# First batch of a fused linear-attention and MLP kernel: order of the kv and x products, a one-column mean operand, evictions split over two engines, float32 fill matmuls

## The chip, the cores and the metric

The kernel runs on one core of one Trainium2 chip. The metric is the device time of one execution, in microseconds (us), smaller being better. Instructions run on five engines, each with its own queue in program order: PE (TensorE, matmuls; PEld in the profile is its loading of the stationary operand, which runs beside the matmul before it), DVE (VectorE), ACT (ScalarE), POOL (GpSimd) and SP (SyncE). POOL and SP mostly issue DMA transfers here.

## What is computed

```
q_s = softmax(q, over head_dim)            # 8 batches, 8 heads, 576 tokens, 64
k_s = softmax(k, over the tokens)
kv  = einsum('bhsd,bhse->bhde', k_s, v)    # one 64 x 64 matrix per head
x   = einsum('bhsd,bhde->bhse', q_s, kv)   # heads side by side: 576 x 512
xn  = (x - mean(x)) / sqrt(var(x) + 1e-6) * g_ln
out = x + relu(xn @ w_ch1) @ w_ch2         # 512 x 2048 and 2048 x 512
```

## The kernel before

Each batch has 576 tokens: 512 are handled batch by batch in four tiles of 128 tokens (t = 0 to 3), and the last 64 of all batches together at the end. Two heads share a block of 128 columns, so there are four head pairs (j = 0 to 3) and four blocks of 128 rows of w_ch1 (ko = 0 to 3). All of the work is put in order by hand: `run` walks the list of main matmul steps of a batch and calls side work at given places in it. After the first batch, PE has work nearly all the time.

The change lies in `first_batch` (line 957), which does what comes before the first MLP, and in the helpers it calls:

- **Loads.** SP issues the first two token tiles of q and then k (lines 978 to 982). POOL first copies four numbers of q into `gate` (line 1004), so that its own transfers start when that q has landed, and then issues in this order: v in three parts (line 1006: heads 0 to 3, 4 and 5, 6 and 7), q tiles 2 and 3 (line 970), the first 512 columns of w_ch1 in two halves of K (line 1013: ko 0 and 1, then ko 2 and 3; tile `w_raw`), the other column blocks of w_ch1 (line 99), w_ch2 (line 103) and batch 1.
- **Fill.** `warm(n)` (line 863) issues n matmuls of 128x512 on the zeroed tile `junk`, with nothing depending on them.
- **q.** `exp_qt` (ACT, line 220), then for tiles 0 and 1 `norm_q` (DVE, lines 229, 274, 923), then `eq_pT`: four PE transposes into the PSUM tile `ptr` (line 928) and a copy to `eqT` on DVE (line 934) or ACT (line 930). Tiles 2 and 3 are not divided by their sums; those come later from `z_q` (PE line 940, DVE line 943).
- **k and kv.** `exp_k0` (ACT, line 293), `z0_mm` (PE, line 306: the sums of k), `g_columns` (line 953, a float32 matmul that transposes g), `recip_z`. `kv0_mm(j)` does six matmuls for a head pair (line 321); DVE scales and masks the result into `kv_sb` and sums its rows into a column (line 322). That column is then spread into a 128x128 tile `mbc`: by ACT (line 327) for j = 0 to 2, by DVE (line 331) for j = 3. `mbc` is all `-1/512` (`ones_w`) times the sum, so that a matmul with it as stationary operand subtracts the mean of x.
- **x, transposed.** `xT_mm(j, kh)` (line 342) adds pair j's share to one PSUM tile `pxT` for each half kh of the 512 columns of x: one matmul with `kv_sb` where the pair belongs to the half, and two with `mbc`. `xT_out(i)` multiplies block i by g and writes `xnT`, the moving operand of the MLP: on DVE for i = 0, 1 (line 351), on ACT for i = 2, 3 (line 353). This gives tokens 0 to 255.

The order on PE is kv0_mm(0), (1), (2), xT_mm(0, 0), kv0_mm(3), xT_mm(1, 0), (2, 0), (0, 1), (3, 0), the transposes of q tile 2, xT_mm(1, 1), (2, 1), the transposes of q tile 3, xT_mm(3, 1). ACT evicts the transposes of tile 2, DVE those of tile 3.

Then `run(mlp_steps(0), ...)` starts. Its first main steps are matmuls of line 520 with the first 512 columns of w_ch1: eight with ko 0 and 1, then eight with ko 2 and 3. Between them PE does, in this order: after four matmuls `q0_rest(2)` (lines 940, 943, 414), followed on DVE by `x_fast(0, 2)` (line 464) and `x_normed(2)` (line 475); after eight, `q0_rest(3)`; after twelve, the transposes of the normalized tile 2 (line 928 into `ptr`, evicted by DVE at line 932), then `x_fast` and `x_normed` of tile 3. The next main steps are sixteen matmuls of 128 columns for tile 2, the transposes of tile 3, and sixteen matmuls with the second column block of w_ch1.

Of the kernel before, what the change touches and what calls it, by code (L numbers as in the profile page):

```python
# [12 lines left out]
FP32 = mybir.dt.float32  # L13
BF16 = mybir.dt.bfloat16
AF = mybir.ActivationFunctionType
# [5 lines left out]
def kernel(  # L21
# [16 lines left out]
    nc = tc.nc  # L38

    B, H, S, D = q.shape  # L40
    DM = H * D
    DH = 4 * DM
    P = 128
    T = 4
# [4 lines left out]
    NP = H // 2  # L49
# [10 lines left out]
    const = ctx.enter_context(tc.tile_pool(name="const", bufs=1))  # L60
# [12 lines left out]
    eps_ln = const.tile([P, 1], FP32)  # L73
    gate = const.tile([P, 4], FP32)
    ones = const.tile([P, 1], BF16)
    junk = const.tile([P, P], BF16)
    scrap = const.tile([P, 512], BF16)
    bones = const.tile([P, 2], BF16)
    ones_w = const.tile([P, P], BF16)
    diag = const.tile([P, P], FP32)  # L80
    mbc = const.tile([P, NP, P], BF16)
    g_one = const.tile([P, KO1], FP32)
    w1_sb = wts.tile([P, KO1, DH], BF16, name="w1_raw")
    w1g = const.tile([P, KO1, DH], BF16)
# [12 lines left out]
    def load_w1(nb):  # L97
        cols = slice(nb * 512, nb * 512 + 512)
        nc.gpsimd.dma_start(w1_sb[:, :, cols], w1_src[:, :, cols])
# [100 lines left out]
    def new_eq(c):  # L200
        eqs[c] = (
            att.tile([P, T, H, D], BF16, tag="eq", name="eq", bufs=1),
            sml.tile([P, T, H], FP32, tag="zq", name="zq"),
            sml.tile([P, T, H], FP32, tag="rq", name="rq"),
        )
        eqTs[c] = att.tile([P, T, NP, P], BF16, tag="eqT", name="eqT")
# [10 lines left out]
    def exp_qt(b, t):  # L217
        if t == 0 and b:
            new_eq(b)
        nc.scalar.activation(eqs[b][0][:, t], raws[b][2][:, :, t], AF.Exp)  # L220
# [66 lines left out]
    kvbox = {}  # L287
# [9 lines left out]
    def k0_mm(j, t):  # L297
        hs = slice(2 * j, 2 * j + 2)
        return eks[0][0:P0, t, hs, :], raws["v0"][0:P0, hs, t, :], P
# [16 lines left out]
    def kv0_mm(j):  # L316
        pool, tag = (att_ps, "a") if j < 2 else (mm_ps, "m")
        pkv = pool.tile([P, P], FP32, tag=tag, name="pkv")
        for t in range(T0):
            lhsT, rhs, w = k0_mm(j, t)  # L320
            nc.tensor.matmul(pkv[:, 0:w], lhsT, rhs, start=(t == 0), stop=(t == T0 - 1))
        nc.vector.scalar_tensor_tensor(
            kv_sb[:, 0, j, :], in0=pkv, scalar=kvbox["rz"][:, j : j + 1], in1=diag,
            op0=ALU.mult, op1=ALU.mult, accum_out=kvbox["sum"][:, j : j + 1],
        )
        if j < NP - 1:
            nc.scalar.activation(
                mbc[:, j], ones_w, AF.Copy, scale=kvbox["sum"][:, j : j + 1]
            )
        else:  # L330
            nc.vector.tensor_scalar_mul(
                out=mbc[:, j], in0=ones_w, scalar1=kvbox["sum"][:, j : j + 1]
            )

    def xT_mm(j, kh):

        if j == 0:
            pobox["T", kh] = mm_ps.tile([P, 2, 2, P], FP32, tag="m", name="pxT")
        ops = [(kv_sb[:, 0, j, :], j % 2)] if j // 2 == kh else []
        ops += [(mbc[:, j], i) for i in range(2)]  # L340
        for n, (lhsT, i) in enumerate(ops):
            nc.tensor.matmul(
                pobox["T", kh][:, i], lhsT, eqTs[0][:, 0:2, j, :],
                start=(j == 0 and n == 0), stop=(j == NP - 1 and n >= len(ops) - 2),
                skip_group_check=True,
            )

    def xT_out(i):
        dst, src = xnTs[0][:, 0:2, i, :], pobox["T", i // 2][:, i % 2]
        if i < 2:  # L350
            nc.vector.tensor_scalar_mul(out=dst, in0=src, scalar1=g_one[:, i : i + 1])
        else:
            nc.scalar.activation(dst, src, AF.Copy, scale=g_one[:, i : i + 1])
# [509 lines left out]
    def warm(n):  # L863

        w = mm_ps.tile([P, 4, P], FP32, tag="m", name="warm")
        for _ in range(n):
            nc.tensor.matmul(w, junk, junk[:, 0:4].to_broadcast([P, 4, P]), start=True, stop=True)
# [57 lines left out]
    def pe_T(dst, src, t, eng, scale=None):  # L925
        ptr = mm_ps.tile([P, NP, 2 * P], BF16, tag="m", name="ptr")
        for j in range(NP):
            nc.tensor.transpose(ptr[:, j, 0:P], src[:, j * P : j * P + P], ident)  # L928
        if eng is nc.scalar:
            nc.scalar.copy(dst[:, t], ptr[:, :, 0:P])  # L930
        elif scale is not None:
            nc.vector.tensor_mul(dst[:, t], ptr[:, :, 0:P], scale.to_broadcast([P, NP, P]))
        else:
            nc.vector.tensor_copy(out=dst[:, t], in_=ptr[:, :, 0:P])
# [10 lines left out]
    def eq_pT(c, t, eng):  # L945
        pe_T(eqTs[c], eqs[c][0][:, t].rearrange("p h d -> p (h d)"), t, eng)
# [10 lines left out]
    def first_batch():  # L957

        nc.scalar.preload_act_table_set("natural_log_exp_and_others")
        raws[0] = (  # L960
            mlp.tile([P, H, T0, D], FP32, tag="hT", name="kt0", bufs=1), None,
            raw.tile([P, H, T, D], FP32, tag="qt", name="qt"),
        )
        k0, _, q0 = raws[0]
        v0 = mlp.tile([P, H, T0, D], BF16, tag="hs", name="v0", bufs=1)
        raws["v0"] = v0

        def load_q0(t, tn, eng):
            ts = slice(t, t + tn)
            eng.dma_start(  # L970
                q0[:, :, ts],
                q[0, :, 0:SM, :].rearrange("h (p t) d -> p h t d", t=T)[:, :, ts],
            )

        def src0(x, h0, hn):
            return x[0, h0 : h0 + hn].rearrange("h (p t) d -> p h (t d)", t=T0)

        load_q0(0, 2, nc.sync)
        for h0 in range(0, H, 2):
            nc.sync.dma_start(  # L980
                k0[0:P0, h0 : h0 + 2].rearrange("p h t d -> p h (t d)"), src0(k, h0, 2)
            )
        raws["g"] = outp.tile([KO1, P], FP32, tag="ot", name="g_rows")
        nc.scalar.dma_start(
            raws["g"], bass.AP(moe_g_ln.tensor, moe_g_ln.offset, [[P, KO1], [1, P]])
        )
        nc.vector.memset(junk, 0.0)
        nc.vector.memset(eps_ln, 1e-6)
        nc.vector.memset(ones, 1.0)
        nc.vector.memset(bones, 0.0)  # L990
        nc.vector.memset(bones[0:64, 0:1], 1.0)
        nc.vector.memset(bones[64:P, 1:2], 1.0)
        nc.vector.memset(ones_w, -1.0 / DM)
        nc.vector.memset(diag, 0.0)
        for ps in halves:
            nc.vector.memset(diag[ps, ps], 1.0)
        nc.vector.memset(kv_sb[:, 1:B], 0.0)
        nc.vector.memset(vr, 0.0)
        for half in range(2):
            nc.vector.memset(vr[64 * half : 64 * half + 64, :, 4 * half : 4 * half + 4, D:], 1.0)  # L1000
        nc.vector.memset(vm[:, :, :, :, D:], 1.0)
        make_identity(nc, ident)
        nc.gpsimd.tensor_copy(out=ident_f, in_=ident[0:KO1, 0:KO1])
        nc.gpsimd.tensor_copy(out=gate, in_=q0[:, 1, 0, 0:4])
        for h0, hn in ((0, 4), (4, 2), (6, 2)):
            nc.gpsimd.dma_start(  # L1006
                v0[0:P0, h0 : h0 + hn].rearrange("p h t d -> p h (t d)"), src0(v, h0, hn)
            )
        for t in range(2, T):
            load_q0(t, 1, nc.gpsimd)  # L1010
        for kh in range(2):
            ks = slice(2 * kh, 2 * kh + 2)
            nc.gpsimd.dma_start(w1_sb[:, ks, 0:512], w1_src[:, ks, 0:512])
        for nb in range(1, 4):
            load_w1(nb)
        load_w2(0)
        load_w2(1)

        new_eq(0)
        start_x(0)  # L1020
        warm(17)
        for t in range(2):
            exp_qt(0, t)
            norm_q(0, t)
        eq_pT(0, 0, nc.vector)
        warm(6)
        eq_pT(0, 1, nc.vector)
        for j in range(NP):
            exp_k0(j)
            z0_mm(j)  # L1030
            if j == NP - 2:
                g_columns()
        recip_z()
        kv0_mm(0)
        kv0_mm(1)
        kv0_mm(2)
        xT_mm(0, 0)
        kv0_mm(3)
        exp_qt(0, 2)
        exp_qt(0, 3)  # L1040
        xT_mm(1, 0)
        xT_mm(2, 0)
        xT_mm(0, 1)
        xT_mm(3, 0)
        xT_out(0)
        xT_out(1)
        eq_pT(0, 2, nc.scalar)
        xT_mm(1, 1)
        xT_mm(2, 1)
        eq_pT(0, 3, nc.vector)  # L1050
        xT_mm(3, 1)
        xT_out(2)
        xT_out(3)

    def q0_rest(t):
        z_q(0, t)
        for i in range(NP):
            po_mm(0, t, i)
# [132 lines left out]
```

## Time and profile before

The medians and the profile are of the same kernel; the profiled execution is one more run.

| | us |
|---|---|
| median of 3 runs (lowest, highest) | 262.51 (261.97, 262.89) |
| profiled execution | 262.09 |
| its span, first to last instruction | 260.3 |
| PE busy in the span | 253.9 (98%) |
| DVE, ACT, POOL busy | 223.1 (86%), 177.5 (68%), 103.2 (40%) |
| PE instructions (matmuls; loads) | 2885; 2885 |

Times of rows are counted from the start of the span. A row of a timeline has start, length, engine, line, operation, `out<-in`, shape and count; in square brackets stands how long the engine had been idle before and what ended it. The length of a matmul row includes the time in which its result drains, while the next matmul already runs, so the distance between two starts tells what a matmul costs in a stream: 0.109 us for 256 columns, 0.056 for 128, 0.025 for one or two columns.

### The profile page before, as it was taken

The page shows a single profiled execution, that of the slowest core. Times are in us where ns is not written, and L with a number is a line of the kernel's source. Part 1 is how long each engine was busy: PE and PEld are TensorE (multiplying, and loading weights), DVE is VectorE, ACT ScalarE, POOL GpSimd, SP SyncE. Part 2 cuts the span into 40 slices and gives each one's busy share as a digit, 9 for nine tenths or more (in the row PEclk, how much of TensorE's full clock was granted, in tenths as well). Part 3 has the DMA queues.
Part 4 walks back from the last instruction along what each step waited for, and adds up shares of the span by engine and source line. Part 5 has one row for each costly group of instructions (what it writes and reads, how often), then busy time and mean ns, then how long its engine had stood idle before and what let it go on. Part 6 is the DMA issues. An engine that isn't in the chain of part 4 may idle for free.

```text
span 260.3 us, 7286 instructions
## 1 busy us (share of the span) xinstructions
PE 253.9 (98%) x2885; PEld 215.6 (83%) x2885; DVE 223.1 (86%) x542; ACT 177.5 (68%) x348; POOL 103.2 (40%) x160
## 2 busy tenths in 40 slices
PE   8899999999999999999999999999999999999993
PEld 3689755788888888888888988888889888888883
DVE  6768996989989998899889988998899889957873
ACT  4747790997988685888588858885788386647400
POOL 3953247410299409800980098008200900190000
PEclk9999999999999999999999999999999999999999
DMA  6999999988699995999699859989902630422014
GB/s 198 257 203 208 354 221 332 257 169 308 118 122 321 268 120 107 300 247 107 142 300 235 86 135 304 232 89 161 279 0 50 142 137 1 77 71 99 3 40 121
DMA packets 82618, 45.04 MB, mean 173 GB/s; under 512 B 58196, under 2 KB 79192, under 8 KB 82584
## 3 DMA queue, kind: packets, MB, share of 16 engines
q0 software_dynamic: 32464, 21.76, 45.8%
q1 hardware_dynamic: 49488, 22.29, 36.8%
q10 hardware_dynamic: 632, 0.53, 0.7%
q8 instruction: 22, 0.36, 0.6%
q14 instruction: 12, 0.10, 0.1%
HBM read 36.70 MB, written 9.44 MB: 177 GB/s over the span
## 4 chain that ended last, share of the span: by engine, by line
PE 92%; DMA 4%; POOL 2%; DVE 0%; issue 0%
PE ba L604 21%; PE bx L762 20%; PE bb L762 10%; PE ph L520 8%; PE bb L604 6%; PE be L604 5%; PE bc L604 5%; PE pc L556 5%; PE bc L762 5%; DMA w_raw<-in_moe_w_ch_dram 3%; PE pkv L371 2%; DMA qt<-in_q_dram 2%; PE po L403 2%; PE ptr L928 1%; PE po L414 1%; POOL v L1006 1%
## 5 line engine op out<-in xcount | busy, mean ns | idle before, releaser
L604 PEld LDWEIGHTS <-hs 128*128 128x128 bf16 x512 | 49.6, 98 | 6.0
L269 POOL TENSOR_TENSOR tq<-xnT 128x256 bf16<-128x256 bf16 x30 | 20.1, 671 | 85.3 <-PE bc L604 73.9
L762 PEld LDWEIGHTS <-w_raw 128*128 128x128 bf16 x480 | 46.7, 98 | 5.5
L604 PEld LDWEIGHTS <-hT 128*128 128x128 bf16 x392 | 37.6, 98 | 4.2
L762 PEld LDWEIGHTS <-w1g 128*128 128x128 bf16 x360 | 34.7, 98 | 4.3 <-issue 0.2
L762 PE MATMUL bx<-tq,w_raw 128*128 128x256 bf16 x240 | 31.3, 273 | 0.0
L604 PE MATMUL ba<-w_q,hs 128*128 128x256 bf16 x256 | 30.6, 273 | 0.0
L786 ACT COPY bc<-bx 128x512 f32<-128x512 f32 x30 | 16.7, 596 | 19.1 <-PE bx L762 19.1
L427 ACT ACTIVATE scrap<-x,mv 128x512 bf16<-128x512 bf16 x32 | 23.1, 723 | 4.6 <-DVE mv L457 4.4
L793 DVE TENSOR_TENSOR bb<-bx,s 128x512 f32<-128x512 f32 x30 | 19.5, 694 | 7.2 <-ACT s L790 4.5
L804 ACT ACTIVATE hT<-bb 128x512 bf16<-128x512 f32 x30 | 16.3, 595 | 9.3 <-PE bb L762 9.3
L804 ACT ACTIVATE hT<-bc 128x512 bf16<-128x512 f32 x30 | 16.5, 595 | 8.5 <-PE bc L762 8.5
L796 DVE TENSOR_TENSOR hT<-bx,s 128x512 bf16<-128x512 f32 x30 | 19.3, 684 | 3.2 <-PE bx L762 3.1
L587 DVE TENSOR_TENSOR hs<-hT 128x1024 bf16<-128x1024 bf16 x32 | 21.4, 672 | 0.5 <-ACT hT L804 0.5
L229 DVE TENSOR_REDUCE zq<-eq 128x16 f32<-128x1024 bf16 (+1 forms) x20 | 20.7, 1049 | 0.5 <-ACT eq L220 0.5
L269 POOL TENSOR_TENSOR tq<-xnT,tq 128x256 bf16<-128x256 bf16 x30 | 20.0, 669 | 1.1
L449 DVE SCALAR_TENSOR_TENSOR x<-po,rq 128x256 bf16<-128x256 f32 x48 | 17.5, 420 | 1.7 <-PE po L403 1.7
L790 ACT COPY s<-bb 128x512 f32<-128x512 f32 x30 | 16.6, 622 | 0.0
L804 ACT ACTIVATE hT<-bx 128x512 bf16<-128x512 f32 x30 | 16.4, 610 | 0.0
L762 PE MATMUL bx<-xnT,w1g 128*128 128x256 bf16 x120 | 16.2, 273 | 0.0
L762 PE MATMUL bx<-tq,w1g 128*128 128x256 bf16 x120 | 15.9, 272 | 0.0
L762 PE MATMUL bc<-xnT,w1g 128*128 128x256 bf16 x120 | 15.8, 273 | 0.0
(157 smaller groups left out, 535.0 us busy)
## 6 DMA issues: line engine op xcount, KB each, us to landing
out_dram<-ot POOLq DMA_DIRECT2D x30, 256.0 KB, 4.4
kt<-in_k_dram SPq DMA_DIRECT2D x5, 1024.0 KB, 11.6
qt<-in_q_dram SPq DMA_DIRECT2D x4, 1024.0 KB, 9.9
qt<-in_q_dram POOLq DMA_DIRECT2D x2, 1024.0 KB, 12.7
kt<-in_k_dram POOLq DMA_DIRECT2D x2, 1024.0 KB, 14.5
vm<-in_v_dram POOLq DMA_DIRECT2D x16, 128.0 KB, 12.4
qt<-in_q_dram SPq DMA_DIRECT2D x3, 512.0 KB, 5.7
w_raw<-in_moe_w_ch_dram POOLq DMA_DIRECT2D x3, 512.0 KB, 10.5
```

Of the source, the lines that this page charges most:

```text
L229: nc.vector.reduce_sum(eqs[c][1][:, ts], eqs[c][0][:, ts], axis=AX.X)
L269: nc.gpsimd.tensor_tensor(out=dst[:, t], in0=x[:, t], in1=y[:, t], op=ALU.subtract)
L427: nc.scalar.activation(scrap, x[:, t], AF.Square, bias=mv[:, t, 0:1], scale=-float(DM), accum_out=mv[:, t, 1:2],)
L449: nc.vector.scalar_tensor_tensor(x[:, t].rearrange("p (i two d) -> p i two d", two=2, d=D)[:, :, half], in0=pobox[c, t][half], scalar=1.0, ...
L520: nc.tensor.matmul(ph[:, m % 2, at : at + tn], (w1g if c else w1_sb)[:, ko, m * P : (m + 1) * P], xnTs[c][:, t0 : t0 + tn, ko, :], start=( ...
L587: nc.vector.tensor_tensor(out=dst, in0=x, in1=y, op=op)
L604: nc.tensor.matmul(hbox[bank][:, t, cs], lhsT, rhs[:, cs], start=first and (own or t == 0) and k == 0, stop=k == KH - 1, skip_group_check= ...
L762: nc.tensor.matmul(dst[:, q], lhsT, rhs, start=first and q == 0 and ko == 0, stop=ko == 1, skip_group_check=True)
L786: nc.scalar.copy(at[g, "c"], at[g, "x"])
L793: nc.vector.tensor_tensor(out=at[g, "b"], in0=at[g, "x"], in1=at[g, "s"], op=ALU.add)
L796: nc.vector.tensor_tensor(out=h_out(g, 1, 1), in0=at[g, "x"], in1=at[g, "s"], op=ALU.add)
L804: nc.scalar.activation(h_out(g, odd, half), at[g, name], AF.Relu)
```

## The change

It touches the first batch alone.

- The fill matmuls use a float32 `junk`; there are 4 and 1 of them in place of 17 and 6.
- The mean is kept as one column per pair (`kvm`, the sum times -1/512), and a matmul reads that column 128 times with step 0 as its stationary operand; the 128x128 tiles `mbc` and `ones_w` go.
- All four `kv0_mm` come ahead of every `xT_mm`; the `xT_mm` of half 0 come together, then those of half 1, and the transposes of q tiles 2 and 3 come after both.
- In each half DVE evicts the first block and ACT the second.
- `exp_qt(0, 3)` comes after the evictions of half 0 on ACT, and DVE evicts the transposes of both q tiles.

```diff
-    junk = const.tile([P, P], BF16)
+    junk = const.tile([P, P], FP32)
...
-    ones_w = const.tile([P, P], BF16)
...
-    mbc = const.tile([P, NP, P], BF16)
+    kvm = const.tile([P, NP], BF16)
...
+        total = kvbox["sum"][:, j : j + 1]
         if j < NP - 1:
-            nc.scalar.activation(
-                mbc[:, j], ones_w, AF.Copy, scale=kvbox["sum"][:, j : j + 1]
-            )
+            nc.scalar.activation(kvm[:, j : j + 1], total, AF.Copy, scale=-1.0 / DM)
         else:
-            nc.vector.tensor_scalar_mul(
-                out=mbc[:, j], in0=ones_w, scalar1=kvbox["sum"][:, j : j + 1]
-            )
+            nc.vector.tensor_scalar_mul(out=kvm[:, j : j + 1], in0=total, scalar1=-1.0 / DM)
...
-        ops += [(mbc[:, j], i) for i in range(2)]
+        ops += [(kvm[:, j : j + 1].to_broadcast([P, P]), i) for i in range(2)]
...
-        if i < 2:
+        if i % 2 == 0:
...
-        nc.vector.memset(ones_w, -1.0 / DM)
...
-        warm(17)
+        warm(4)
...
-        warm(6)
+        warm(1)
...
-        kv0_mm(0)
-        kv0_mm(1)
-        kv0_mm(2)
-        xT_mm(0, 0)
-        kv0_mm(3)
+        for j in range(NP):
+            kv0_mm(j)
         exp_qt(0, 2)
-        exp_qt(0, 3)
-        xT_mm(1, 0)
-        xT_mm(2, 0)
-        xT_mm(0, 1)
-        xT_mm(3, 0)
+        for j in range(NP):
+            xT_mm(j, 0)
         xT_out(0)
         xT_out(1)
-        eq_pT(0, 2, nc.scalar)
-        xT_mm(1, 1)
-        xT_mm(2, 1)
-        eq_pT(0, 3, nc.vector)
-        xT_mm(3, 1)
+        exp_qt(0, 3)
+        for j in range(NP):
+            xT_mm(j, 1)
         xT_out(2)
         xT_out(3)
+        for t in range(2, T):
+            eq_pT(0, t, nc.vector)
```

## The prediction

> **What bounds the kernel now.** First the page: which engine is full, and which ends the chain.
>
> ```profile
> PE 253.9 (98%) x2885; PEld 215.6 (83%) x2885; DVE 223.1 (86%) x542; ACT 177.5 (68%) x348; POOL 103.2 (40%) x160
> ...
> PE 92%; DMA 4%; POOL 2%; DVE 0%; issue 0%
> ```
>
> PE bounds the time, so an edit pays only if PE begins its long run earlier or stands still less. The share that is not PE lies at the start, so the second view is the chain that ended last, in order of time (start, length):
>
> ```profile
> 7.33 1.84 POOL qt L970 x2
> 9.18 0.64 POOL w_raw L1013
> 9.82 6.86 DMA w_raw<-in_moe_w_ch_dram
> 16.72 0.61 PE ph L520 x4
> ```
>
> Up to 16.72 us nothing that PE, DVE or ACT computes is on the chain. It waits for the second half of the first w_ch1 block, which POOL issues at 9.82 and which lands at 16.68. All edits lie before that. The third view, the PE timeline, tells how much earlier PE could have gone on:
>
> ```profile
> 11.31 0.27 PE L342 MATMUL pxT<-eqT,kv_sb 128*128 128x256 bf16 x1
> 11.60 0.39 PE L342 MATMUL pxT<-eqT,mbc 128*128 128x256 bf16 x2
> 11.83 0.50 PE L321 MATMUL pkv<-v,ek 96*128 96x128 bf16 x6
> ...
> 15.93 0.38 PE L414 MATMUL po<-kv_sb,eqT 128*128 128x128 bf16 x4
> 16.72 0.61 PE L520 MATMUL ph<-xnT,w_raw 128*128 128x256 bf16 x4 [0.41 <-DMA w_raw<-in_moe_w_ch_dram]
> ```
>
> The last `po` starts at 16.09, so PE is free at 16.15 and 0.57 us are lost. The fourth, DVE's timeline, shows the chain behind the stall:
>
> ```profile
> 15.34 0.21 DVE L943 RECIPROCAL rq<-zs 128x8 f32<-128x8 f32 x1 [0.42 <-PE zs L940]
> 15.66 0.69 DVE L464 SCALAR_TENSOR_TENSOR x<-po,rq 128x512 bf16<-128x512 f32 x1
> 16.28 0.08 DVE L464 DVE_READ_ACCUMULATOR x<-po,rq 128x1 f32 x1
> 16.40 0.35 DVE L475 TENSOR_SCALAR xn<-x,st 128x512 bf16<-128x512 bf16 x1
> ...
> 17.60 0.69 DVE L932 TENSOR_TENSOR xnT<-ptr,g_col 128x512 bf16<-128x512 bf16 x1 [0.73 <-PE ptr L928]
> ```
>
> `xn` of tile 2 is ready at 16.75, before PE asks for it at 17.17. From there DVE and PE alternate until 19.57, where the second w_ch1 block is needed; it landed at 19.26.
>
> Last, the DMA view of 15 to 17 us:
>
> ```profile
> q0 software_dynamic: 394, 0.40, 120.8%
> q8 instruction: 1, 0.02, 3.0%
> ```
>
> The engines are full. Of the sixteen landing marks of that `w_raw` half, fifteen are there by 15.71; the last comes at 16.68. The packet in q8 has 16 KB, starts at 15.90 and takes 0.95 us. There are 22 such packets for 5784 PE records, one per 263, and this first one starts when PE has begun 260. I read it as PE's own instructions, fetched on an engine that still had weights to deliver. For the half before, the last mark came 0.18 behind the next to last; undisturbed, this one would be there at 15.71 + 0.18 = 15.89.
>
> **Fill.** 23 bf16 matmuls become 5 in float32. Nothing depends on them, and after each lot PE waits for DVE (line 923 ends at 7.36 and 8.92). The one float32 matmul of the trace, `gcp`, makes two records, each with a load of 0.18 us. So `warm(4)` is 8 records. A 512-column record costs 0.427 before 4.2 us (distance of the loads) and 0.218 after. With one pass per record the fill, begun at 1.0, ends at 4.5; with two at 6.1, as it does now (6.3); all slow, at 7.9. The first two are hidden; the last delays the first transposes by 0.5, but DVE copies those at 8.84 only. I take 0, with two passes, since 16 passes are nearest to the 17 of now. The Trainium skill, FP8 and Floating Point Precision, "TensorE Precision Notes", has true FP32 take four passes, which would be two per record; no run shows it yet, and the sum would stay as it is. What counts is that 46 fill records become 20: PE's stream is 26 shorter.
>
> **Mean column.** ACT's three `mbc` (1.17 together) become 128x1 operations: not under 0.2 (line 505, 128x4: 0.21), not over 0.39; I take 0.21. DVE's 0.25 becomes 0.14 (line 482, 128x1). A load with step 0 is not in the trace: 0.098 as other loads (nothing to gain, it lies under the matmul before it, 0.109), at most 0.18 as float32. I take 0.098; the tile is bf16 as they are. At 0.18, sixteen loads cost 16 x 0.07 = 1.1. The `ones_w` memset (0.17) goes and `junk` takes 0.06 more; both are hidden by the first q transfer (5.03).
>
> **The new order**, from the same rows. Part 3 of v lands at 11.72, so `kv0_mm(3)`, before at 11.83, starts at 11.77 and PE idles from 11.31, where `xT_mm(0, 0)` stood: the order gives that filling away. Last kv matmul 12.05; `kv_sb(3)` 0.25 later, 12.31 to 12.67 with its sum; `kvm(3)` at 12.84. `xT` half 0 runs from 12.11, ten at 0.109, its last start at 13.09, result 0.31 later at 13.40 (before 13.51). DVE and ACT evict side by side, to 13.86. `exp_qt(0, 2)` (q landed at 12.42, 0.72) is done by 13.16; `exp_qt(0, 3)` runs behind the eviction, 13.78 to 14.50 (before 13.84). `xT` half 1: last start 14.18, evicted 14.49 to 14.95. Transposes of tile 2 from 14.29, of tile 3 from 14.56. DVE has `xT_out(2)` ahead of them: copies to 15.29 and 15.63 (before 14.92 for the later). Then PE: four `ph` 14.79 to 15.23, waits for `eqT` of tile 2, `zs` and `po` 15.34 to 15.66, four `ph` to 16.10, `zs` and `po` of tile 3 to 16.42. So PE is free at 16.42, 0.27 **later** than before; the DMA wait covers that. On DVE: `rq` 15.62, `x` 15.87, its sum to 16.57, `xn` 16.62 to 16.97 (before 16.75). Queued behind it is only `rq` of tile 3. No DMA is moved; POOL and SP issue as before, and batch 1's k, which reuses the tile of `ek`, is queued to 15.09 behind POOL's own issues.
>
> **The instruction packet.** In the old stream its trigger lies some time before 15.90, say at record 210 to 245 (14.1 to 15.4). The same place in the new stream is 26 records later in the work, at 15.4 to 16.5: the packet starts at about 17, and `w_raw` lands at 15.9. Then PE goes on at 16.42 and reaches the transposes of tile 2 at 16.86, where `xn` (16.97, plus 0.05) is late next: 17.02 in place of 17.17. All behind moves by 0.15, to 19.42 at the second block, which may still land at 19.26 with the packet on its engine.
>
> The Trainium skill, Runtime: NRT & Kernel Launch, "Instruction fetch mechanics", calls the cost of crossing an instruction block mostly hidden. For PE's own issue that agrees with this trace; the 0.8 us on the weights' last mark (16.68 - 15.89) speaks against it. By that rule alone the change would give 0.
>
> **Sum.** Fill 0, column 0, order 0 (its +0.27 is under the wait), packet -0.15: the profiled execution goes from 262.09 (span 260.3 and 1.8 around it, unchanged) to 261.94. The median shown is 0.42 above that execution; 262.51 - 0.15 = 262.36.
>
> **Rivals.**
> - *The transfer hides everything.* The packet still meets the same half, landing stays at 16.68, PE (16.42) and `xn` (16.97, asked at 17.17) stay under it: 262.5. For it: the trigger is inferred. 0.26.
> - *Slower: the clock.* Loads stand 0.427 apart until 3.96 and 0.218 from 4.31: PE runs at half speed until it has worked some 3.2 us. If float32 fill does not count as work, the rise comes 3.2 us after the dense matmuls begin at 10.2. Then 3.2 us of work, half done, lose 1.6; 0.3 of slack before 16.72 and some 0.3 of v's wait take up 0.6: +1.0, 263.5. It decides as soon as more than 0.6 us are lost. If it comes only after the line 520 stream, some +4.5. Against it: two passes per record keep PE as busy as now. 0.10. The Trainium skill, TensorE: Matmul & The Clock Gate, "Part 1: The HAM clock gate", has the full rate return after one busy window of about 3.4 us and be lost after an idle one; the rise at 4.2 us agrees.
> - *Slower: the step-0 load* is at 0.18: PE free at 17.5, +0.8, 263.3. It costs from 0.02 per load on (0.3 / 16). 0.05.
> - *Later packets.* All 21 others move by 26 records; each can hold a transfer for 0.9 us or free one. Either sign, mostly under 0.5; PE has some 3 us of stalls behind 19.6 in all. 0.17: 0.07 faster by over 0.8, 0.03 slower by that, the rest between.
>
> **Numbers.** Forecast 0.42. 0.3% is 0.79 us, about what a measurement of this kernel can tell from no change. Faster: 0.07, and 0.02 for a forecast whose DVE chain is shorter than worked out: 0.09. Slower: 0.10 + 0.05 + 0.03 = 0.18, less 0.01 for the load's lower half: 0.17. Same: 0.74. Range: forecast and first rival with 0.7 either way, and up to the near end of the clock rival: 261.6 to 263.4.
>
> **What would show it.** Right: no PE row with a DMA wait at 16.7; line 520's second lot at about 16.4; line 928 on `xn` at 17.0; the q8 packet after 16.4. The order: `pkv` idle before 11.77, `pxT` half 0 done at 13.4, DVE's `eqT` copies at 14.9 and 15.2. Step-0 loads of 98 ns. Ten float32 records, full rate by 4.2 us. Wrong: 16.72 unchanged; matmuls 0.21 apart behind 10 us; loads over 0.12; any new PE idle behind 20 us.

## The result, and the profile after

The changed kernel takes 263.94 us (median of 7 runs, 263.21 to 264.76), the kernel before 262.44 on the same chip: ratio 1.006 [1.0037, 1.0083]. It is slower by 1.5 us where 262.36 was forecast; the forecast range ended at 263.4. The profiled execution took 264.76, with a span of 263.0.

The page of the changed kernel, first as a whole: busy time, the granted clock in 40 slices, and the two queues that carry data (packets, MB, share of 16 engines' time).

```profile
PE 256.1 (97%) x2872; PEld 216.7 (82%) x2872; DVE 223.4 (85%) x542; ACT 176.6 (67%) x347; POOL 103.1 (39%) x160
...
PEclk9979999999999999999999999999999999999999
...
q0 software_dynamic: 32464, 21.76, 46.1%
q1 hardware_dynamic: 49488, 22.29, 38.5%
```

PE has fewer records and yet 2.2 us more of work: the clock row has a 7 in its third slice. And q1, SyncE's queue, moves what it moved before, 49,488 packets and 22.29 MB, but for 38.5% of a longer span; before it was 36.8%. That row is the key to the case, and it is easily passed over, because no transfer was edited.

The chain that ended last, in order of time, up to 18 us (start, length, what):

```profile
0.74 4.54 DMA qt<-in_q_dram
...
6.93 5.65 DMA v<-in_v_dram
12.58 0.05 issue
12.62 0.70 PE pkv L320 x6
13.32 3.67 PE pxT L338 x20
16.99 0.03 issue
17.02 0.48 DVE xnT L347
17.50 0.66 DVE eqT L930 x2
```

Before, these 18 us ended in a wait for `w_raw`. That wait is gone; the chain now runs through `v`, which lands at 12.58 (before 11.72), and through twenty `x` matmuls that take 3.67 us; at the pace of before, 0.109, they would take 2.2. The PE timeline of the same stretch:

```profile
12.62 0.70 PE L320 MATMUL pkv<-v,ek 96*128 96x128 bf16 x6 [0.49 <-DMA v<-in_v_dram]
...
13.97 2.34 PE L338 MATMUL pxT<-eqT,kvm 128*128 128x256 bf16 x10
16.10 0.33 PE L338 MATMUL pxT<-eqT,kv_sb 128*128 128x256 bf16 x1
...
17.30 0.60 PE L516 MATMUL ph<-xnT,w_raw 128*128 128x256 bf16 x4
...
18.99 0.60 PE L516 MATMUL ph<-xnT,w_raw 128*128 128x256 bf16 x4
```

Ten matmuls begin at 13.97 and the next at 16.10, so they stand 0.213 apart, twice the 0.109 of before: half clock. Four consecutive stretches show it (stretch, length, busy time of PE, PEld, DVE, ACT and POOL with their counts, granted clock, DMA share, GB/s):

```profile
5.97:9.39 3.42, 2.69 (x12) 0.84 (x11) 3.28 (x7) 2.87 (x4) 3.42 (x6) 1.00 1.14 248
9.39:12.80 3.41, 2.56 (x51) 2.27 (x50) 1.98 (x11) 1.60 (x5) 3.41 (x6) 1.00 1.24 234
12.80:16.21 3.41, 3.41 (x21) 2.54 (x19) 1.00 (x4) 0.82 (x2) 2.84 (x5) 0.50 1.18 205
16.21:19.60 3.39, 3.38 (x43) 2.62 (x41) 2.42 (x8) 1.27 (x3) 1.47 (x2) 1.00 1.24 206
```

The clock is full from 5.97, half for exactly one stretch of 3.41 us, and full again. In the stretch ahead of the fall PE was busy for 2.56 of 3.41 us. Counted from the rise of the clock, that is the second stretch of 3.41 us. The second one of before, where the clock rose at 4.22, has PE busy for 3.42 of 3.42:

```profile
7.63:11.05 3.42, 3.42 (x54) 2.46 (x52) 2.69 (x10) 2.03 (x3) 3.42 (x5) 1.00 1.28 221
```

The busy time alone doesn't decide, though. In another execution of the changed kernel (e16 below) the clock rose at 6.56, and its second stretch is hardly fuller, yet the clock stayed up behind it:

```profile
9.97:13.39 3.42, 2.61 (x37) 2.25 (x38) 1.77 (x11) 1.39 (x4) 3.42 (x6) 1.00 1.20 241
```

What sets the two apart is taken up with the counts of the falls.

So there are two losses to explain. That second profile (`e16_after_again`), without a fall, parts them: its span is 261.7, against 260.3 before and 263.0 here. Some 1.4 us are there without any fall, and the fall adds 1.3.

### The profile page after: what moved, and what is told of

Same layout as the page of the kernel before. It is cut to its first block, busy times and chain, and to the rows that moved or that the text cites. A ratio compares the mean times of both kernels' runs of the same rounds, so it can differ in the third digit from the quotient of the medians.

```text
span 263.0 us, 7259 instructions
## 1 busy us (share of the span) xinstructions
PE 256.1 (97%) x2872; PEld 216.7 (82%) x2872; DVE 223.4 (85%) x542; ACT 176.6 (67%) x347; POOL 103.1 (39%) x160
## 3 DMA queue, kind: packets, MB, share of 16 engines
q1 hardware_dynamic: 49488, 22.29, 38.5%
## 4 chain that ended last, share of the span: by engine, by line
PE 93%; DMA 4%; DVE 1%; POOL 1%; issue 0%; DVEq 0%
PE ba L600 21%; PE bx L758 20%; PE bb L758 10%; PE ph L516 8%; PE bb L600 6%; PE be L600 5%; PE bc L600 5%; PE pc L552 5%; PE bc L758 5%; DMA v<-in_v_dram 2%; PE pkv L367 2%; DMA qt<-in_q_dram 2%; PE po L399 2%; PE pxT L338 1%; PE ptr L924 1%; PE po L410 1%
## 5 line engine op out<-in xcount | busy, mean ns | idle before, releaser
L758 PE MATMUL bx<-xnT,w1g 128*128 128x256 bf16 x120 | 16.2, 273 | 0.0
L758 PE MATMUL bx<-tq,w1g 128*128 128x256 bf16 x120 | 15.9, 272 | 0.0
## 6 DMA issues: line engine op xcount, KB each, us to landing
kt<-in_k_dram POOLq DMA_DIRECT2D x2, 1024.0 KB, 15.9
```

The lines of the kernel that those rows point to most:

```text
L758: nc.tensor.matmul(dst[:, q], lhsT, rhs, start=first and q == 0 and ko == 0, stop=ko == 1, skip_group_check=True)
```

## The experiments

No kernel leaves out any of the computation. "Before" is the kernel before on the same chip, in the same rounds. "Clock up" is the median of the runs whose mean granted clock shows no fall (above 0.9945), with their number and that of the runs with a fall. "Start" is where the tiles that the first transfers write (batch 0's q, k and v, and the one tile that holds all of `w_ch1`) begin in a partition of SBUF, modulo 256 bytes, from the built program; in e14 the `w_ch1` tile begins at 0 and the others at 32. "q1" is the share of 16 engines' time that SyncE's queue takes in the first 12 us for the same 1,872 packets.

| run | start | us | before | ratio [95%] | clock up (up, fell) | q1 |
|---|---|---|---|---|---|---|
| before | 0 | | 262.28 to 262.55 | | 262.28 to 262.44 (124, 15) | 50.6% |
| after | 32 | 263.94 | 262.44 | 1.006 [1.0037, 1.0083] | 263.41 (4, 3) | 55.7% |
| e1 after, bf16 fill | 32 | 263.52 | 262.28 | 1.0047 [1.0024, 1.007] | 263.48 (8, 4) | 58.0% |
| e2 before, f32 fill | 0 | 262.41 | 262.28 | 0.9999 [0.9979, 1.0018] | 262.32 (11, 1) | 49.9% |
| e3 after, own banks | 32 | 264.30 | 262.28 | 1.006 [1.0036, 1.0084] | 263.34 (3, 6) | 57.4% |
| e4 before, column | 32 | 263.44 | 262.28 | 1.0042 [1.0025, 1.006] | 263.43 (10, 2) | 58.1% |
| e5 after, 64 B | 64 | 264.28 | 262.42 | 1.0053 [1.0035, 1.0071] | 262.98 (3, 7) | 55.5% |
| e6 before, 32 B | 32 | 263.44 | 262.42 | 1.0031 [1.0013, 1.0048] | 263.24 (9, 2) | 55.8% |
| e7 column, 64 B | 64 | 263.17 | 262.42 | 1.0019 [1.0003, 1.0034] | 263.17 (12, 0) | 56.0% |
| e8 e7 and f32 fill | 64 | 264.04 | 262.42 | 1.0052 [1.0031, 1.0073] | 263.81 (2, 4) | 56.9% |
| e9 after, 256 B | 0 | 262.64 | 262.55 | 1.0007 [0.998, 1.0033] | 262.52 (7, 5) | 49.9% |
| e10 column, 256 B | 0 | 262.29 | 262.55 | 0.9988 [0.9962, 1.0013] | 262.28 (11, 1) | 50.4% |
| e11 e10 and f32 fill | 0 | 262.73 | 262.55 | 1.0008 [0.9976, 1.004] | 262.68 (11, 1) | 50.4% |
| e12 before, 128 B | 128 | 263.27 | 262.55 | 1.0005 [0.998, 1.0031] | 263.14 (10, 2) | 54.2% |
| e13 constants only | 0 | 262.58 | 262.38 | 1.0008 [0.9994, 1.0022] | 262.57 (12, 0) | 50.8% |
| e14 data only | 32 | 263.73 | 262.38 | 1.005 [1.0034, 1.0065] | 263.73 (6, 0) | 57.9% |
| e15 e9, own banks | 0 | 262.91 | 262.38 | 1.0027 [1.0, 1.0053] | 262.47 (7, 5) | 48.4% |
| e16 after again | 32 | 264.66 | 262.38 | 1.0087 [1.0072, 1.0102] | 263.49 (1, 6) | 58.0% |
| e17 e15, bf16 fill | 0 | 262.36 | 262.33 | 1.0017 [0.9998, 1.0037] | 262.29 (9, 3) | 48.1% |
| e18 column, other pads | 0 | 262.29 | 262.33 | 0.9985 [0.9959, 1.001] | 262.29 (12, 0) | 51.9% |

The last column splits without overlap: 48.1 to 51.9% where the start is a multiple of 256, 54.2 to 58.1% elsewhere.

**First, the parts by themselves.** The theories were (1) the thin float32 fill lets the clock fall, and (2) the two evictions of `x` take turns where side by side was assumed.

```diff
# e1, in after
-    junk = const.tile([P, P], FP32)
+    junk = const.tile([P, P], BF16)
-        warm(4)
+        warm(17)
...
-        warm(1)
+        warm(6)
```

> The changed kernel with the bf16 fill of before (17 and 6 matmuls); all else as changed. Theory 1 (thin fill lets the clock fall): no run has a stretch at half clock behind 10 us, the slow third of the runs (264.3 to 264.8) is gone, median 263.4. Rival (the clock falls because of the new order, which leaves PE waiting for v and for the evictions): the clock still falls in some runs, median about 263.9. Theory 2 (two evictions of one PSUM tile run one after the other) is untouched here: ACT's eviction still starts when DVE's ends, and 1.0 us over before remain. Packet theory: PE's first instruction packet is back at about 16 us and again meets a w_ch1 transfer.

```diff
# e2, in before: the reverse
-    junk = const.tile([P, P], BF16)
+    junk = const.tile([P, P], FP32)
-        warm(17)
+        warm(4)
...
-        warm(6)
+        warm(1)
```

> The kernel before with only the float32 fill (4 and 1). Theory 1 in its strong form (float32 fill does not hold the clock): the clock falls in about 4 runs of 10, those take 263.5, the median is 262.8. If the order is needed too: no fall, 262.4. Packet theory: the first instruction packet comes 26 records later, the second w_ch1 half lands without its straggler, line 520 goes on at 16.2 in place of 16.7, and the time is up to 0.37 us under before: 262.1.

```diff
# e3, in after: one PSUM tile for each half of x
-            pobox["T", kh] = mm_ps.tile([P, 2, 2, P], FP32, tag="m", name="pxT")
+            for i in range(2):
+                pobox["T", kh, i] = mm_ps.tile([P, 2, P], FP32, tag="m", name="pxT")
```

> The changed kernel with a PSUM tile of its own for each of the four blocks of x, so that DVE and ACT read different tiles. Theory 2 (the shared PSUM tile makes ACT wait for DVE): both evictions of a half start within 0.1 us of each other, exp_qt of q tile 3 comes 0.5 us earlier, and the time falls by 0.5 to 1.0 us, to 263.0 to 263.4 in the median (clock falls of theory 1 stay). Rival (both write one xnT tile, and that is what ACT waits for): ACT still starts behind DVE, time as changed, 263.9.

```diff
# e4, in before: the column alone, old order, old fill
-    ones_w = const.tile([P, P], BF16)
-    mbc = const.tile([P, NP, P], BF16)
+    kvm = const.tile([P, NP], BF16)
```

> The kernel before with only the one-column mean operand read with step 0. All theories: loads of 98 ns, the three ACT operations 0.2 us each in place of 0.4, time 262.4, within 0.2 of before. If a load with step 0 were slow (0.18 us), 263.3 and loads of that length in the trace.

e1 is still slower (1.0047), e2 is not (0.9999): the fill by itself is not the loss. Nor does the fall go with it, as theory 1 had it: 4 of e1's 12 runs still show one. e3 gains nothing: theory 2 falls as a price. e4 was meant as the harmless part and is slower by 1.2 us, with the old order and the old fill. The step-0 loads were not it: all 16 were as short as any other (e10's rows are below). What was late in e4 were the transfers: `k` parts 1.16 apart where before has 1.02. The `kvm` tile is 8 bytes wide and takes the place of 1,280, and every tile allocated behind it moves. Allocation goes pool by pool, so the raw q, k, v and weight tiles went from a multiple of 256 bytes to 32 past one.

**Second, theory 3: the tiles' addresses.** Its test is e6: the instructions of before, with one unrelated tile 32 bytes longer.

```diff
# e6, in before
-    gate = const.tile([P, 4], FP32)
+    gate = const.tile([P, 12], FP32)
...
-        nc.gpsimd.tensor_copy(out=gate, in_=q0[:, 1, 0, 0:4])
+        nc.gpsimd.tensor_copy(out=gate[:, 0:4], in_=q0[:, 1, 0, 0:4])
```

> The kernel before with the tile gate at 48 bytes per partition in place of 16 (only the first 16 used): all tiles behind it start 32 bytes later, at 32 modulo 64; the same instructions. Address theory: k parts 1.13 us apart from the start, line 520's first lot at about 16.0 in place of 14.6, time 263.4, as the column alone. Rival (the column): 262.3, nothing moves.

```diff
# e5, in after: multiples of 64 bytes
-    kvm = const.tile([P, NP], BF16)
+    kvm = const.tile([P, 8 * NP], BF16)
```

> The changed kernel with a kvm tile of 64 bytes per partition in place of 8 (a slot of 32), of which the first columns are used; every tile behind it then starts at a multiple of 64 bytes again, as before, and nothing else differs. Address theory (the smaller mean tile moved all later SBUF tiles, q, k, v and w_raw among them, to 32 modulo 64, and transfers into them are slower): the k parts land 1.02 us apart as before, not 1.13, v's third part at about 11.7, the second w_ch1 half by 16.0; the time falls by 1.0 to 1.3, to 262.6 to 262.9, or lower by the packet's 0.1. Rival (the one-column operand itself, its loads or its small operations, costs the time): transfers as in the changed kernel, time 263.9.

e7 is e4 with e5's line, e8 is e7 with e2's fill.

> The kernel before with the one-column operand, its tile at 64 bytes so that later tiles stay at multiples of 64. Address theory: 262.3, the column itself is free (within 0.2 of before). Rival (the column costs): 263.4 as with the tile of 8 bytes.

> The kernel before, in its old order and with its old evictions, with the aligned one-column operand and the float32 fill: all of the change but the order. Address theory with the packet theory: k parts 1.02 apart, the first instruction packet at about 16.7 and no straggler of the second w_ch1 half, line 520's second lot at 16.1; 262.0 to 262.4. If the order was what cost: the same. Rival (column): 263.4.

e6 is slower by 1.02 us (1.0031 [1.0013, 1.0048]) and does nothing else than before. Its `exp` operations on ACT stand behind the four parts of `k`; here are the rows of before and, in the second fence, of e6 (start, length, then in brackets the idle time and what ended it):

```profile
6.11 0.82 ACT L293 ACTIVATE ek<-kt 96x768 bf16<-96x768 f32 x1
7.13 0.84 ACT L293 ACTIVATE ek<-kt 96x768 bf16<-96x768 f32 x1 [0.20 <-DMA kt<-in_k_dram]
8.16 1.82 ACT L293 ACTIVATE ek<-kt 96x768 bf16<-96x768 f32 x2 [0.19 <-DMA kt<-in_k_dram]
```

```profile
6.39 0.84 ACT L293 ACTIVATE ek<-kt 96x768 bf16<-96x768 f32 x1
7.52 0.84 ACT L293 ACTIVATE ek<-kt 96x768 bf16<-96x768 f32 x1 [0.29 <-DMA kt<-in_k_dram]
8.64 0.84 ACT L293 ACTIVATE ek<-kt 96x768 bf16<-96x768 f32 x1 [0.29 <-DMA kt<-in_k_dram]
9.74 0.84 ACT L293 ACTIVATE ek<-kt 96x768 bf16<-96x768 f32 x1 [0.26 <-DMA kt<-in_k_dram]
```

The same operation, waiting 0.29 in place of 0.20 for each part. Theory 3 stands, but its form, multiples of 64 bytes, fell: e5, e7 and e8 start at such multiples and are slower all the same.

**Third, which multiple.** e9 is after with `kvm` as `[P, 32 * NP]` (256 bytes), e10 is e4 with that line, e11 is e10 with e2's fill, e12 is before with `gate` as `[P, 36]`, which moves the tiles by 128.

> The changed kernel with a kvm tile of 256 bytes per partition (first columns used), so that the tiles behind it start at multiples of 256 bytes, as they do in the kernel before. Address theory, mended (the step that matters is 128 or 256 bytes, not 64): k parts 1.02 us apart, v's third part at 11.7, the clock falls seldom, line 520 begins at about 15; time 262.4 to 262.8: nearly the whole loss goes, and what is left is the order with its evictions in turn. Rival (order, evictions and fill cost it): k parts at 1.02 but time 263.3 or more. If the addresses have no part: 263.9, k parts at 1.13.

> The kernel before with the one-column operand and its tile at 256 bytes; later tiles start at multiples of 256. Address theory: k parts 1.02 apart, time as before, 262.3 to 262.5. Rival (column costs): 263.2 to 263.4 as with 8 or 64 bytes.

> The kernel before with one-column operand (256 bytes) and float32 fill: the change without its order and evictions. Address theory: k parts 1.02 apart, no straggler of the second w_ch1 half, line 520's second lot at 16.1, few clock falls; 262.0 to 262.4. If the float32 fill alone made the clock fall: 4 in 10 runs at half clock for one stretch, 263.5 for those.

> The kernel before with the tile gate at 144 bytes (first 16 used): all later tiles start 128 bytes later, at 128 modulo 256; same instructions. If the step is 256 bytes: k parts 1.08 to 1.13 apart, time 262.9 to 263.4. If it is 128 bytes: 1.02 apart and 262.4.

With 256 bytes the loss is gone: e9 1.0007, e10 0.9988, e11 1.0008, none of them to be told from before. e9 has every instruction of the change, float32 fill, column and new order, and with the clock up it takes 262.52, where after takes 263.41. e12's interval includes no change; its clock-up median (263.14 against 262.44) and its q1 share put it with the slow ones. Here is the DMA view of the first 12 us, q1's row, in the order before, e10, after, e14 (described below), one fence for each:

```profile
q1 hardware_dynamic: 1872, 1.70, 50.6%
```

```profile
q1 hardware_dynamic: 1872, 1.70, 50.4%
```

```profile
q1 hardware_dynamic: 1872, 1.70, 55.7%
```

```profile
q1 hardware_dynamic: 1872, 1.70, 57.9%
```

Same packets, same bytes; a packet takes 0.506 x 16 x 12 us / 1872 = 51.9 ns before and 57.1 in after. More traffic beside them isn't the reason: in these 12 us the other data queue, q0, moves 1.02 MB in before and 0.76 in after.

**Fourth, which tiles.** e13 shifts the constants by 32 bytes and, with a pad of 224 bytes ahead of the `w_ch1` tile, brings that tile and the data behind it back to a multiple of 256. e14 leaves the constants and the `w_ch1` tile and shifts the rest.

```diff
# e13, in before, with gate [P, 12] as in e6
+    wpad = wts.tile([P, 112], BF16, name="wpad")
     w1_sb = ...
# e14, in before
     w1_sb = ...
+    wpad = wts.tile([P, 16], BF16, name="wpad")
```

> The kernel before with its constant tiles (w2_sb, w1g, kv_sb, vm and so on) 32 bytes later and w_raw and all tiles behind it (q, k, v, eqT, xnT) at multiples of 256 again. If it is the target address of the early transfers that counts: k parts 1.02 us apart, 262.4 as before. If operands that engines read from the constant tiles count: 262.8 or more.

> The kernel before with constants and w_raw where they were and the tiles of q, k, v, eqT, xnT and all behind them 32 bytes later. Target-address theory: k parts 1.10 to 1.15 apart, v's third part at 12.3 or later, line 520's first lot at 15.7; 263.0 to 263.4 without a clock fall. Rival (constants or w_raw): 262.4.

e15 is e9 with e3's own PSUM tiles, e16 is after, unchanged.

> The changed kernel with kvm at 256 bytes and a PSUM tile for each block of x, so that both evictions of a half start together. If the evictions in turn cost something once transfers are fast: 0.3 less than with 256 bytes alone, 262.2 to 262.3, and line 520's first lot at 14.8 in place of 15.3. If the w_ch1 transfer hides them: the same 262.5.

> The changed kernel as it is, on the chip of the other three. Address theory: k parts 1.13 apart, 1.0 to 1.2 over before in runs whose clock stays up, and over 2 in those where it falls for a stretch behind 10 us; 4 to 7 runs in 10 fall. If the clock depends on the chip more than on the kernel: as many falls in the kernels with fast transfers beside it.

e14 carries the whole loss (+1.35, 1.005 [1.0034, 1.0065]); in e13 the +0.2 is not resolved. In e16 the change costs 1.0087 [1.0072, 1.0102]; six of its seven runs show a fall. Its PE timeline, in which the clock stayed up, shows where the time goes without a fall:

```profile
12.52 0.51 PE L320 MATMUL pkv<-v,ek 96*128 96x128 bf16 x6 [0.26 <-DMA v<-in_v_dram]
...
15.96 0.60 PE L516 MATMUL ph<-xnT,w_raw 128*128 128x256 bf16 x4
...
20.32 0.40 PE L924 MATMUL ptr<-ident,xn 128*128 128x128 bf16 x4
20.55 0.93 PE L516 MATMUL ph<-xnT,w_raw 128*128 128x256 bf16 x7
```

The second `w_ch1` block lands at 20.43 (before 19.26), and its matmuls begin at 20.55 (before 19.57): 0.98 of the 1.4 us are lost by there. The addresses alone do about as much: in e6 and e14, with the old order, that block lands at 20.26 and 20.45, and its matmuls begin at 20.39 and 20.82, 0.82 and 1.25 later than in before.

**Last, the order and the clock.** e17 is e15 with e1's bf16 fill. e18 is e4 with `kvm` as `[P, 208]` and a `wpad` of `[P, 48]` ahead of `w1_sb`: the early targets keep their multiples, and `w2_sb`, at 96 past a multiple of 256 in before, goes to one as well.

> The changed order with the mean column, kvm at 256 bytes, a PSUM tile per block of x and the bf16 fill of before: the change with its addresses mended and its fill undone. If the float32 fill is what lets the clock fall: falls as seldom as before (1 in 10 or less), median 262.4. If the new order (PE waits for v with nothing else to do) does it: falls in 3 or more of 10, 264.0 for those; the rest 262.4 to 262.5.

> The kernel before with the mean column and with w2_sb, too, at a multiple of 256 bytes (in the kernel before it starts at 96 modulo 256, while w_raw, q, k and v start at 0). If addresses of later transfers count as well: DMA has more room from 17 to 45 us and the time is 0.1 to 0.3 under before, 262.1. If only what PE waits for counts: 262.3, as with the column at 256 alone.

e17, the new order on good addresses, takes 262.36 against 262.33. e18 takes as long as e10 (262.29; 0.9985 [0.9959, 1.001]), so the later target `w2_sb` brings nothing that shows. No version is shown to beat the kernel before.

**The falls of the clock**, counted over all runs:

| order, fill, start | falls |
|---|---|
| before | 15 of 139 |
| old, bf16, 0 (e10, e13, e18) | 1 of 36 |
| old, f32, 0 (e2, e11) | 2 of 24 |
| old, bf16, not 0 (e4, e6, e7, e12, e14) | 6 of 53 |
| new, bf16, 0 (e17) | 3 of 12 |
| new, f32, 0 (e9, e15) | 10 of 24 |
| new, bf16, not 0 (e1) | 4 of 12 |
| old, f32, not 0 (e8) | 4 of 6 |
| new, f32, not 0 (after, e3, e5, e16) | 22 of 33 |

Neither the float32 fill alone nor the slow transfers alone make falls more frequent than before. Together they do, and the order isn't needed for it: e8 is e7 with that fill, and falls in 4 of 6 runs where e7 falls in 0 of 12. With the new order the two fall in 22 of 33, and the fill and the order on good addresses in 10 of 24. The rate differs between chips, too: the kernel before fell in 8 of 35 runs on the one that ran e9 to e12, and in 7 of 104 on the other three. A fall costs 1.3 in after (264.70 against 263.41), 1.1 to 1.5 in e3, e5, e9 and e15, 0.9 in e1 and 1.9 in e17. How much belongs to the order and how much to the fill on good addresses is open: 3 of 12 (e17) against 10 of 24 doesn't tell them apart.

The traces show more of when it falls. In the 20 profiles here the clock rises between 3.91 and 6.82 us, and six show a fall (after, e3, e5, e8, e9, e15). In all six it begins 6.83 us behind the rise, two stretches of 3.41, as in after from 5.97 to 12.80. So chance can enter with the rise: it sets which matmuls lie in the second stretch. Counted by the columns that PE moves in that stretch (a float32 record twice), the six have 1,576 to 2,856 and the other fourteen 3,368 to 6,660; after has 2,856 and e16, with the same instructions, 4,366. At 0.109 us for 256 columns, 2,856 are 1.2 us of work in 3.41. No run set the number of columns to test this, so it stands as what these 20 profiles agree in, not as a rule that is shown.

## Why the prediction was wrong

**The step that failed** is the assumption beneath every landing time: "Part 3 of v lands at 11.72", `w_raw` at 15.9, the second block at 19.26, since "No DMA is moved; POOL and SP issue as before". The issues were as before. The targets were not: two constant tiles went, an 8-byte one came, and all that is allocated behind them began 32 bytes past a multiple of 256. Part 3 of v landed at 12.58 (12.47 with the clock up), the second block at 20.32 (20.43). No rival had this. It costs 1.0 to 1.1 us by clock-up medians (263.41 against 262.3 to 262.4), 0.9 against e9, which differs from the changed kernel in nothing but the addresses, and 0.8 to 1.4 in e6 and e14, which change no operation of the work. The rest of the 1.5 comes from the falls, which raise the median of all runs from 263.41 to 263.94.

**Fill: cost right, side effect missed.** Two passes per float32 record was right. The load rows of the changed kernel stand 0.855 apart at half clock, twice 0.427:

```profile
2.07 0.34 PEld L863 LDWEIGHTS warm<-junk 128*128 128x128 f32 x1 [0.52 <-issue]
2.92 0.34 PEld L863 LDWEIGHTS warm<-junk 128*128 128x128 f32 x1 [0.52 <-issue]
```

The Trainium skill, FP8 and Floating Point Precision, "TensorE Precision Notes", with its four passes for a float32 matmul, agrees: two records of two passes each. As forecast it is hidden (e2: 0.9999). It ends at 7.2, not 6.1, since the clock rose at 5.97 here.

**The clock rival** had the price (+1.0 forecast, 1.3 measured) and its sign (matmuls 0.21 apart behind 10 us; they stand 0.213 apart) but not the mechanism. It let a fill that doesn't count as work delay the rise. No such delay shows: the clock rises at 4.18 to 6.56 us in the nine profiles with the float32 fill and at 3.91 to 6.82 in the eleven with bf16, so the 4.2 of the prediction was one execution's. What comes is a fall later on, behind a stretch in which PE waits for `k` and `v` and in which the new order leaves it nothing else to do, as forecast for 11.31 to 11.77. That wait was priced as idle time only. The Trainium skill, TensorE: Matmul & The Clock Gate, "Part 1: The HAM clock gate", has the full rate lost after an idle window of about 3.4 us; the length agrees (3.41), but here the window was busy for 2.56 of 3.41 us and the clock fell. By columns it held 1.2 us of work.

**Column: right.** Its rows in e10, where nothing else is changed:

```profile
L338 PEld LDWEIGHTS <-kvm x16: 95/98/100, 11.5 to 14.2; 128*128 128x128 bf16 x16
...
L327 ACT ACTIVATE kvm<-kvs x3: 206/206/207, 11.2 to 11.9; 128x1 bf16<-128x1 f32 x3
L329 DVE TENSOR_SCALAR kvm<-kvs x1: 156/156/156, 12.7 to 12.7; 128x1 bf16<-128x1 f32 x1
```

98 ns for the step-0 load as forecast, 0.206 and 0.156 for 0.21 and 0.14.

**Evictions "side by side": wrong, and it cost nothing that shows.** ACT's eviction waits for DVE's, since both read one PSUM tile. The rows of the changed kernel, DVE's, then ACT's:

```profile
15.50 0.48 DVE L347 TENSOR_SCALAR xnT<-pxT,g_one 128x256 bf16<-128x256 f32 x1 [1.58 <-PE pxT L338]
```

```profile
16.01 0.47 ACT L349 ACTIVATE xnT<-pxT,g_one 128x256 bf16<-128x256 f32 x1 [1.85 <-DVE xnT L347]
```

With a PSUM tile for each (e15) ACT's releaser is PE, and it starts 0.22 behind DVE:

```profile
16.55 0.47 ACT L352 ACTIVATE xnT<-pxT,g_one 128x256 bf16<-128x256 f32 x1 [1.66 <-PE pxT L340]
```

The time is the same: 262.47 against 262.52 (e15, e9, clock up). In e16 the turn is on the chain ahead of `eqT` of tile 3, but the second `w_ch1` block, landing at 20.43 for matmuls at 20.55, leaves 0.12 to be gained.

**The instruction packet: right in place, without a gain.** It moved out of the `w_raw` half's way, to 17.57 in after and 16.73 in e2. In e2, which has the 26 records less and nothing else, the half landed at 15.99 and line 520's second lot began at 16.10 (forecast 15.9, and 16.2 in that run's expectation):

```profile
16.10 0.60 PE L520 MATMUL ph<-xnT,w_raw 128*128 128x256 bf16 x4
16.76 0.40 PE L928 MATMUL ptr<-ident,xn 128*128 128x128 bf16 x4
```

The profiled span was shorter by 0.38, but the median was 262.41 against 262.28: a gain of 0.15 is under what these runs can tell, and the later packets moved too. So the rival in which the edits bring nothing is right in its number for this part, though not in its cause, a packet that stays.

**Order: right in its steps where a trace has them undisturbed, without a gain.** In e17, whose `v` is on time (11.56, where 11.72 was forecast), the `x` matmuls begin at 11.96 and the last one at 14.03; forecast were 12.11 and 14.18, so both are 0.15 early, as `v` is. Behind them that profile waits for a late `w_ch1` transfer, and the other profiles of the order have slow or late transfers from the start, so the forecast of 16.42 for a free PE can't be read off. With addresses mended the whole change is within 0.1 us of before by clock-up medians (262.52 and 262.44), where 0.15 less was forecast. Over all runs, falls included, e9 is at 1.0007 [0.998, 1.0033] and e15 at 1.0027 [1.0, 1.0053].

## What to carry to other kernels

An edit that resizes or removes a tile moves every tile behind it: look up where the transfers' targets begin before and after, and keep them on multiples of 256 bytes, or an instruction-level comparison charges the edit with the transfers' slowdown (here about 1 of 1.5 us). Compare the time that a queue takes for the same packets in the same stretch; it showed here within one profile what medians needed many runs for. And work that seems free to shift, such as filling on PE while it waits for data, may hold the clock up: price its absence as a chance of a stretch at half clock, not as idle time alone.

## What the runs showed of the hardware

- Transfers into SBUF take longer where their target doesn't begin at a multiple of 256 bytes: 49.3 to 53.2 ns for a q1 packet at multiples of 256, 55.6 to 59.6 at 32, 64 and 128 past one (share x 16 x 12 us / 1872). The Trainium skill, DMA: Bandwidth & Descriptors, "How a descriptor splits into AXI transactions", has a descriptor cut into transactions that begin at multiples of 256 bytes; where it begins elsewhere, the first one starts at the multiple below, and the bytes ahead of the descriptor's start are fetched unused. The step of 256 agrees; the page tells it of reads, while here the written side moved, so the mechanism inside the engine isn't shown.
- A moved `w_ch1` tile isn't needed for the loss: e14 left that tile, which holds all of `w_ch1`, on its multiple, moved q, k, v and all behind them, and is slower by 1.35 us. What moving `w_ch1` alone would cost wasn't run.
- The clock can fall for a stretch of 3.41 us, or two (e9, e15), behind a stretch in which PE counts as busy three quarters of the time; in all six profiles the fall begins 6.83 us behind the rise. With the same busy share it also stayed up (e16): the columns moved tell the two apart, at most 2,856 where it fell and at least 3,368 where it didn't. Falls show in 15 of 139 runs of the kernel before, and in 22 of 33 of the changed order and fill on slow addresses.
- In the profiles of e9 and e15 `v` landed at 13.14 and 13.17 on good addresses (before 11.72), and the clock was at half for two stretches behind it. In e17's, `v` is on time (11.56), but the first half of the first `w_ch1` block lands at 15.96 (before 14.37). Why these were late isn't settled; all three executions took longer than their kernels' medians, by which the comparisons above go.
